# Attention and two feed-forward layers in float32 from float64 weights: the weight decode split over ScalarE and one VectorE step, decoded weights kept in PSUM

## The chip, the core and the metric

One core of a Trainium2 chip runs the whole program. Its engines work side by side and meet at semaphores: TensorE (PE, with its weight loads shown apart as PEld), VectorE (DVE), ScalarE (ACT), GpSimd (POOL) and SyncE (SP), which issues the transfers. Each engine runs its own list of instructions strictly in order. The metric is the device time of one execution in microseconds (us); lower is better.

## The reference, cut to what matters

```python
attn = softmax(causal(q @ k.T / 8)) @ v           # 2 batches x 12 heads x 448 x 64, float32
x    = attn as 896 tokens x 768
xn   = x / sqrt(mean(x*x) + 1e-6) * rms_g
x    = (silu(xn @ w_gate) * (xn @ w_val)) @ w_out          # 768 -> 1536 -> 768
h    = maximum(x @ w_in, 0)                                 # 768 -> 2048
out  = (h * h) @ w2_out                                     # 2048 -> 768
```

The five weight matrices arrive as float64: each number is a pair of 32-bit words, and the kernel has to make float32 of it on the chip. Activations are float32.

## The kernel before, in words

**Precision.** Every float32 operand of the large products is split into a rounded part (`high`, type float32r) and the rest (`low`), and three matmuls of 128x128 by 448 columns replace one. For an activation this is `parts` (L483 to L493: `high` through `rnd`, L198 to L204, `low` at L491); for a weight tile it is `form` (L591 to L607: `low` at L603), which writes a buffer of the pool `ring`.

**Decoding.** `weights` (L549 to L589) loads a tile of 128 x 768 float64 numbers as pairs of words into `raw` and makes float32 of it in `wt`, in four steps: `exponent` (L563 on ACT or L565 on POOL) reads the high word as a float32 and multiplies it by 2^-112; `sign` (L573 on DVE or L571 on POOL) writes the sign bit back into the high word's place; `upper` (L577, DVE) shifts the result left by three and puts the sign in; `lower` (L581, DVE) adds the top three bits of the low word.

**Products.** `product` (L609 to L621, the matmuls at L617) runs nine matmuls for a form of three 128-row blocks. Two column tiles of a weight matrix and the two batches make a 2x2 block product, done with seven products instead of eight: `differences` (L635 to L656, subtractions at L644) makes sums of activations, `minus` (L624 to L632, at L630) sums of weights, and `halves` (L658 to L699) runs one such pair of tiles: two `weights`, four `minus`, seven `form`, seven `product`, and the evictions in between (`snap` at L243 or L682, and `half_silu` at L711, `gated` at L734 or `squared` at L878). A pair has 63 matmuls. There are ten pairs for gate and value, then `layer` (L840 on) for the first output matrix, eight pairs for the second input matrix, and `layer` again for the last matrix.

**Order.** Nothing is issued in the order in which it is written. `Order` (L44 to L135) holds every step with its due time, the engines that may do it with an estimated duration each (functions A_, D_, P_, E_, L245 to L258), what it needs and which buffers it takes, and `run` plays it through: the step that could begin first is given to the engine with the lowest end plus a penalty (`COST`), and ties within `SLACK` go to the earliest due time. What comes out is one fixed list for each engine. Attention's twelve head pairs (`step`, L266 on) are due 6 us apart (`STRIDE`); the weights of the first tiles are decoded beside them. `norm` scales the finished rows (L540). PSUM is used by the attention pools until `banks_come`, after which eight banks `m` take the products.

## Time and profile before

| what | us |
|---|---|
| median of 3 runs (lowest, highest) | 655.7 (652.54, 658.22) |
| the profiled execution | 651.39 |
| its span, first to last instruction | 649.6 |
| PE busy | 582.8 (90% of the span) |
| DVE busy | 541.3 (83%) |
| POOL busy | 379.7 (58%) |
| ACT busy | 310.1 (48%) |
| mean granted TensorE clock | 0.963 of full |

Busy time is counted by engine over the whole span; what matters is which engine another waits for in each stage. On the page's chain of waits PE has 47% of the span and DVE 42%.

### The profile page before, as it was taken

The page shows a single profiled execution, that of the slowest core. Times are in us where ns is not written, and L with a number is a line of the kernel's source. Part 1 is how long each engine was busy: PE and PEld are TensorE (multiplying, and loading weights), DVE is VectorE, ACT ScalarE, POOL GpSimd, SP SyncE. Part 2 cuts the span into 40 slices and gives each one's busy share as a digit, 9 for nine tenths or more (in the row PEclk, how much of TensorE's full clock was granted, in tenths as well). Part 3 has the DMA queues.
Part 4 walks back from the last instruction along what each step waited for, and adds up shares of the span by engine and source line. Part 5 has one row for each costly group of instructions (what it writes and reads, how often), then busy time and mean ns, then how long its engine had stood idle before and what let it go on. Part 6 is the DMA issues. An engine that isn't in the chain of part 4 may idle for free.

```text
span 649.6 us, 8844 instructions
## 1 busy us (share of the span) xinstructions
PE 582.8 (90%) x3155; PEld 502.9 (77%) x3155; DVE 541.3 (83%) x668; ACT 310.1 (48%) x706; POOL 379.7 (58%) x373
## 2 busy tenths in 40 slices
PE   8998989509997899998899999889898899999997
PEld 5765657409986888787789998678787799999997
DVE  3678788892999999999997789999999999668521
ACT  4888676232454344544523336455555564435200
POOL 3569897571666765668644148767676788236100
PEclk9999999958999999999899999699899999999999
DMA  5365132100232333231345540023333222544111
GB/s 156 90 216 176 58 112 87 61 0 2 80 139 78 104 129 103 98 98 48 97 138 163 185 147 0 21 80 103 133 109 124 81 82 75 161 152 147 39 67 66
DMA packets 19500, 65.06 MB, mean 100 GB/s; under 512 B 2048, under 2 KB 8960, under 8 KB 19456
## 3 DMA queue, kind: packets, MB, share of 16 engines
q1 hardware_dynamic: 19456, 64.50, 30.7%
q8 instruction: 25, 0.41, 0.3%
q14 instruction: 19, 0.16, 0.1%
HBM read 61.74 MB, written 2.75 MB: 99 GB/s over the span
## 4 chain that ended last, share of the span: by engine, by line
PE 47%; DVE 42%; issue 7%; POOL 2%; DMA 1%; ACT 1%; SPq 0%; DVEq 0%; POOLq 0%; ACTq 0%
PE m L617 37%; DVE ring L603 8%; DVE wt L577 5%; DVE wt L581 5%; DVE sb L491 5%; PE s L297 2%; PE t L400 2%; DVE snap L644 2%; DVE fb L722 2%; DVE fa L540 2%; PE o L438 2%; DVE raw L573 2%; DVE st L630 2%; DVE mx L333 1%; PE s L800 1%
## 5 line engine op out<-in xcount | busy, mean ns | idle before, releaser
L617 PE MATMUL m<-sb,ring 128*128 128x448 f32 x1584 | 345.2, 374 | 46.0 <-DVE fa L745 23.3
L617 PEld LDWEIGHTS m<-sb,ring 128*128 128x128 f32 x1584 | 302.9, 193 | 79.7 <-ACT sb L202 23.7
L617 PE MATMUL m<-sa,ring 128*128 128x448 f32 x630 | 143.9, 375 | 6.8 <-DVE ring L603 3.0
L617 PEld LDWEIGHTS m<-sa,ring 128*128 128x128 f32 x630 | 120.9, 193 | 20.5 <-DVE ring L603 5.4
L202 ACT CAST ring<-wt 128x384 fp32r<-128x384 f32 (+1 forms) x107 | 51.6, 501 | 85.8 <-DVE wt L581 43.3
L577 DVE SCALAR_TENSOR_TENSOR wt<-wt,raw 128x768 uint32<-128x768 uint32 x70 | 82.7, 1181 | 5.8 <-POOL raw L571 3.7
L581 DVE SCALAR_TENSOR_TENSOR wt<-raw,wt 128x768 uint32<-128x768 uint32 x70 | 81.0, 1157 | 1.8
L603 DVE TENSOR_TENSOR ring<-wt,ring 128x384 fp32r<-128x384 f32 x77 | 57.7, 762 | 16.3 <-ACT ring L202 15.4
L563 ACT ACTIVATE wt<-raw 128x768 f32<-128x768 f32 (+1 forms) x55 | 48.7, 886 | 44.8 <-DMA raw<-in_w2o 14.9
L603 POOL TENSOR_TENSOR ring<-wt,ring 128x384 fp32r<-128x384 f32 (+1 forms) x45 | 54.3, 1210 | 20.2 <-ACT ring L202 18.9
L603 DVE TENSOR_TENSOR ring<-st,ring 128x384 fp32r<-128x384 f32 x47 | 42.6, 925 | 5.3 <-ACT ring L202 5.3
L630 POOL TENSOR_TENSOR st<-wt 128x384 f32<-128x384 f32 x17 | 19.6, 1157 | 40.3 <-DVE wt L581 39.7
L573 DVE TENSOR_SCALAR raw<-wt 128x768 uint32<-128x768 uint32 (+1 forms) x40 | 29.9, 747 | 15.2 <-ACT wt L563 13.5
L202 ACT CAST ring<-st 128x384 fp32r<-128x384 f32 x67 | 33.2, 511 | 19.2 <-PE m L617 15.2
L571 POOL TENSOR_SCALAR raw<-wt 128x768 f32<-128x768 f32 (+1 forms) x30 | 33.1, 1103 | 15.5 <-ACT wt L563 14.7
L603 POOL TENSOR_TENSOR ring<-st,ring 128x384 fp32r<-128x384 f32 x25 | 33.0, 1318 | 11.4 <-ACT ring L202 11.0
L333 DVE TENSOR_REDUCE mx<-s 128x2 f32<-128x256 f32 (+2 forms) x36 | 24.0, 685 | 17.4 <-PE s L301 10.7
L384 POOL TENSOR_SCALAR p<-p,r 128x128 f32<-128x128 f32 (+1 forms) x48 | 25.4, 547 | 18.8 <-DVE r L374 17.0
L243 ACT COPY snap<-m 128x448 f32<-128x448 f32 x39 | 20.1, 529 | 23.5 <-PE m L617 20.9
L384 POOL TENSOR_SCALAR p2t<-p2t,r 128x256 f32<-128x256 f32 (+1 forms) x36 | 25.9, 736 | 6.0 <-DVE r L374 5.6
L924 DVE TENSOR_TENSOR fb<-m,fb 128x448 f32<-128x448 f32 x12 | 7.5, 624 | 26.1 <-PE m L617 26.1
L297 PE MATMUL s<-qk 64*128 64x128 f32 (+2 forms) x144 | 27.5, 464 | 1.8 <-DMA qk<-in_qk 1.2
(132 smaller groups left out, 821.8 us busy)
## 6 DMA issues: line engine op xcount, KB each, us to landing
raw<-in_w2i SPq DMA_DIRECT2D x16, 768.0 KB, 4.2
raw<-in_wg SPq DMA_DIRECT2D x12, 768.0 KB, 4.6
raw<-in_wv SPq DMA_DIRECT2D x12, 768.0 KB, 4.6
raw<-in_wo SPq DMA_DIRECT2D x12, 768.0 KB, 4.3
raw<-in_w2o SPq DMA_DIRECT2D x12, 768.0 KB, 4.5
qk<-in_qk SPq DMA_DIRECT2D x11, 448.0 KB, 3.3
raw<-in_w2o SPq DMA_DIRECT2D x6, 512.0 KB, 3.8
out_t<-fb SPq DMA_DIRECT2D x12, 224.0 KB, 1.9
```

Source lines behind the costliest of these rows:

```text
L202: eng.copy(o, i)
L297: nc.tensor.matmul(s[:, h, o:o + n], z["qk"][BOTH[h], 0, qs], z["qk"][BOTH[h], 1, :n], start=True, stop=False)
L384: E(e).tensor_scalar(t, t, z["r"][:, k:k + 1], 1.0, ALU.mult, ALU.mult)
L491: E(e).tensor_sub(bs.tile[:, 1], bf.tile, bs.tile[:, 0].bitcast(F32))
L563: nc.scalar.activation(t, hi, AF.Copy, scale=2.0 ** -112)
L571: nc.gpsimd.tensor_scalar(s.bitcast(F32), t, 0.0, 1.0, ALU.mult, ALU.mult)
L573: nc.vector.tensor_scalar(s, t.bitcast(U32), 0x80000000, None, ALU.bitwise_and)
L577: nc.vector.scalar_tensor_tensor(u, u, 3, br.tile[:, :n * P, 1], ALU.logical_shift_left, ALU.bitwise_or)
L581: nc.vector.scalar_tensor_tensor(u, br.tile[:, :n * P, 0], 29, u, ALU.logical_shift_right, ALU.bitwise_or)
L603: E(e).tensor_sub(br.tile[:, 1, :n], num(), br.tile[:, 0, :n].bitcast(F32))
L617: nc.tensor.matmul(bank.tile[:, :S], bw.tile[:, a, i], x[:, c], start=first and i == 0 and k == 0, stop=last and i == n - 1 and k == 2, sk ...
L630: (E(e).tensor_add if plus else E(e).tensor_sub)(bs.tile, x, y)
```

## The change

The decode has three steps now, two of them on ACT. `exponent` is an ACT step with a two-slope function (Prelu): numbers below zero are multiplied by 2^32 times the scale, which leaves a bit pattern that, once shifted left by three, carries the sign. `lowest` (ACT) takes the top byte of the low word, turns it into the three bits that are wanted and writes them back to the low word's place. `number` (DVE) shifts and joins in one step. After attention, the decoded tile lies in a PSUM pool `w` (two buffers of two banks; the pool `m` goes from eight banks to four), and the second tile of a pair has its first half written to an SBUF buffer of pool `st`, so that no sum reads two PSUM operands. POOL reads no PSUM in this program, so steps that read `w` have lost POOL as an option. Steps that read two SBUF operands on DVE are marked `port`, and the planner lets none of them run beside a POOL step in its plan. The planner's durations, `COST`, `STRIDE` and the due times of evictions (`SOON`) differ; `differences` is due after the first tiles of batch 1 and writes rows of `fa`/`fb`; `half_silu` and `squared` work on the bank itself or take one DVE step for relu and square.

```diff
-STRIDE = 6.0
+STRIDE = 5.5
+SOON = 12.0
-COST = {"D": 1.0, "P": 0.6}
+COST = {"D": 0.3, "P": 0.6}
...
+                    if e == "P" or (e == "D" and t["port"]):
+                        b = max(b, free.get("port", 0.0))
...
+            if e == "P" or (e == "D" and t["port"]):
+                free["port"] = end
...
-    caps = dict(raw=2, wt=3, st=4, ring=8, snap=4, tt=2, uu=2, sa=6, sb=18, fa=14, fb=18, m=8)
+    caps = dict(raw=2, wt=2, st=5, ring=8, snap=4, tt=2, uu=2, sa=6, sb=18, fa=14, fb=18, m=4, w=2)
...
-        return 0.26 + 0.00085 * n + (ACC if acc else 0.0)
+        return 0.18 + 0.00085 * n + (0.08 + ACC if acc else 0.0)
...
-            if e == "A":
-                nc.scalar.activation(t, hi, AF.Copy, scale=2.0 ** -112)
-            else:
-                nc.gpsimd.tensor_scalar(t, hi, 2.0 ** -112, 1.0, ALU.mult, ALU.mult)
-        def sign(e):
...
-        def upper(e):
...
-        def lower(e):
...
+            nc.scalar.activation(bt.tile[:, :n * P], br.tile[:, :n * P, 1].bitcast(F32), AF.Prelu, scale=2.0 ** -112, alpha=2.0 ** 32)
+        def lowest(e):
+            b = br.tile.rearrange("p a b -> p (a b)").bitcast(U8).rearrange("p (a b) -> p a b", b=8)[:, :n * P, 3]
+            nc.scalar.activation(br.tile[:, :n * P, 0], b, AF.Copy, scale=1.0 / 32, bias=-31.0 / 64)
+        def number(a, b, dst=None):
+            def f(e):
+                u = bt.tile[:, a:b].bitcast(U32)
+                nc.vector.scalar_tensor_tensor(dst.tile.bitcast(U32) if dst else u, u, 3, br.tile[:, a:b, 0],
+                                               ALU.logical_shift_left, ALU.bitwise_or)
+            return f
...
-        t = chain(due, {"A": A_(w), "P": P_(w)}, exponent, [t], new=[bt], uses=[br], begin=begin)
-        t = add(due, {"P": P_(w), "D": 0.15 + w / 1700}, sign, [t], uses=[bt, br])
-        t = add(due, {"D": D_(w) + 0.02}, upper, [t], uses=[bt, br])
-        t = add(due, {"D": D_(w) + 0.08}, lower, [t], uses=[bt, br])
-        return bt, t
+        t1 = chain(due, {"A": A_(w)}, exponent, [t], new=[bt], uses=[br], begin=begin,
+                   **({"prev": [late["m"]]} if home == "w" else {}))
+        t2 = add(due, {"A": A_(w)}, lowest, [t], uses=[br])
+        if apart:
+            bs, h = buf("st"), w // 2
+            t = chain(due, {"D": D_(h)}, number(0, h, bs), [t1, t2], new=[bs], uses=[bt, br], port=home != "w")
+            return (bs, 0, t), (bt, h, add(due, {"D": D_(h)}, number(h, w), [t1, t2], uses=[bt, br], port=home != "w"))
+        return bt, add(due, {"D": D_(w)}, number(0, w), [t1, t2], uses=[bt, br], port=home != "w")
...
-        t = chain(due, {"A": A_(w), "P": P_(w)}, high, [t], new=[br], uses=[b])
-        return br, n, add(due, {"P": P_(w, True), "D": D_(w) + 0.05}, low, [t], uses=[b, br])
+        sb = b.pool != "w"
+        t = chain(due, {"A": A_(w), **({"P": P_(w)} if sb else {})}, high, [t], new=[br], uses=[b])
+        return br, n, add(due, {**({"P": P_(w, True)} if sb else {}), "D": D_(w)}, low, [t], uses=[b, br], port=sb)
...
-        k1 = snap(x, p1, due + 1.8)
-        done(0, 0, z, k1[0], [p2, k1[1]], due + 4)
+        k1 = snap(x, p1, due + 1.8 - SOON)
+        done(0, 0, z, k1[0], [p2, k1[1]], due + 4 - SOON, False)
...
+        def src():
+            return bf.tile if keep else bank.tile[:, :S]
         def whole(e):
-            nc.vector.tensor_add(bf.tile, bank.tile[:, :S], snap.tile)
+            nc.vector.tensor_add(src(), bank.tile[:, :S], snap.tile)
...
-        have(ctx.enter_context(tc.tile_pool(name="ps_m", bufs=8, space=PSUM)), "m")
+        have(ctx.enter_context(tc.tile_pool(name="ps_m", bufs=1, space=PSUM)), "m", "w")
...
-    f = differences(xf, 500.0)
+    f = differences(xf, 1012.0)
...
-        def relu(e):
-            nc.scalar.activation(bt.tile, bf.tile if snap else bank.tile[:, :S], AF.Relu)
-        def times(e):
-            E(e).tensor_mul(bf.tile, bt.tile, bf.tile if snap else bank.tile[:, :S])
+        def square(e):
+            nc.vector.scalar_tensor_tensor(bf.tile, bf.tile, 0.0, bf.tile, ALU.max, ALU.mult)
```

Over the whole program the lists hold 762 DVE instructions (670 before), 636 on ACT (624) and 195 on POOL (375); the matmuls are the same in number. The changed file's line numbers differ: L540, L491, L644, L603, L630, L716, L722, L739, L742 and L745 of before are L548, L499, L652, L608, L636, L733, L739, L755, L758 and L761 of the change, and the decode on DVE is L581 in it.

Two places of DVE's list, the engine that PE waits for in them. First, the end of attention: `fa` and `fb` are rows of activations, `sb` their split parts, `snap` a scratch row (before: also the differences), `s` the last attention banks. Before, the six scalings of `norm` (L540) and their first splits stand just ahead of these rows, which run to the step that frees the banks (L745):

```order
L644 TENSOR_TENSOR snap<-fa 128x448
L644 TENSOR_TENSOR snap<-fa,snap 128x448
L722 SCALAR_TENSOR_TENSOR fa<-tt,s 128x448
L491 TENSOR_TENSOR sb<-snap,sb 128x448 x2
L644 TENSOR_TENSOR snap<-fa 128x448
L491 TENSOR_TENSOR sb<-snap,sb 128x448
L644 TENSOR_TENSOR snap<-fa 128x448
L644 TENSOR_TENSOR snap<-fa,snap 128x448
L491 TENSOR_TENSOR sb<-snap,sb 128x448 x2
L644 TENSOR_TENSOR snap<-fa,snap 128x448
L491 TENSOR_TENSOR sb<-snap,sb 128x448
L745 SCALAR_TENSOR_TENSOR fa<-s,fa 128x448
```

The same place in the change, from the first scaling after the mean squares of batch 1 on; L761 is the step that frees the banks:

```order
L548 SCALAR_TENSOR_TENSOR fa<-fa,g_sb,snap 128x448 x3
L499 TENSOR_TENSOR sb<-fa,sb 128x448 x3
L548 SCALAR_TENSOR_TENSOR fa<-fa,g_sb,snap 128x448 x3
L499 TENSOR_TENSOR sb<-fa,sb 128x448 x3
L739 SCALAR_TENSOR_TENSOR fa<-tt,s 128x448
L761 SCALAR_TENSOR_TENSOR fa<-s,fa 128x448
L652 TENSOR_TENSOR fb<-fa,fb 128x448
L652 TENSOR_TENSOR fb<-fa 128x448
L608 TENSOR_TENSOR ring<-wt,ring 128x384 x2
```

The differences (L644, now L652) and their parts have moved from ahead of the step that frees the banks to behind it.

Second, DVE's list in the middle of the gate and value pairs. Before:

```order
L716 TENSOR_TENSOR fb<-m,snap 128x448
L722 SCALAR_TENSOR_TENSOR fb<-tt,m 128x448
L739 SCALAR_TENSOR_TENSOR uu<-m,snap 128x448
L722 SCALAR_TENSOR_TENSOR fb<-tt,fb 128x448
L630 TENSOR_TENSOR st<-wt,st 128x384
L742 TENSOR_TENSOR fb<-fb,uu 128x448
L716 TENSOR_TENSOR fb<-m,snap 128x448
L603 TENSOR_TENSOR ring<-wt,ring 128x384
L603 TENSOR_TENSOR ring<-st,ring 128x384 x3
L722 SCALAR_TENSOR_TENSOR fb<-tt,fb 128x448
L603 TENSOR_TENSOR ring<-wt,ring 128x384
L577 SCALAR_TENSOR_TENSOR wt<-wt,raw 128x768
```

The change, at such a place (the end of a value pair and the start of a gate pair):

```order
L581 SCALAR_TENSOR_TENSOR w<-w,raw 128x768
L755 SCALAR_TENSOR_TENSOR uu<-m,snap 128x448
L758 TENSOR_TENSOR fa<-fa,uu 128x448
L733 TENSOR_TENSOR m<-m,snap 128x448
L581 SCALAR_TENSOR_TENSOR st<-w,raw 128x384
L581 SCALAR_TENSOR_TENSOR w<-w,raw 128x384
L739 SCALAR_TENSOR_TENSOR fa<-tt,m 128x448
L608 TENSOR_TENSOR ring<-w,ring 128x384 x2
L636 TENSOR_TENSOR st<-st,w 128x384 x2
L636 TENSOR_TENSOR st<-w,st 128x384
L608 TENSOR_TENSOR ring<-st,ring 128x384 x2
L733 TENSOR_TENSOR fa<-m,snap 128x448
```

A tile takes one decode step here (or two of half its width), evictions (L733, L755) stand between the decode steps, and five of the seven sums and splits shown read `w`.

## Rows read from the trace of the kernel before

**Rows 1.** Windows by stage: us, busy (instructions) of PE, PEld, DVE, ACT, POOL; clock; DMA.

```profile
44.00:122.10 78.10, 70.60 (x590) 50.53 (x586) 65.40 (x111) 52.22 (x159) 60.80 (x79) 1.00 0.36 112
122.10:145.40 23.30, 0.00 (x0) 0.00 (x0) 23.08 (x22) 9.17 (x17) 18.94 (x15) 0.61 0.00 1
145.40:329.70 184.30, 169.23 (x782) 149.76 (x782) 169.29 (x194) 81.41 (x162) 112.66 (x95) 0.97 0.26 86
329.70:404.70 75.00, 75.00 (x369) 69.20 (x369) 61.63 (x68) 30.56 (x57) 33.93 (x30) 1.00 0.43 137
404.70:518.20 113.50, 99.06 (x435) 86.67 (x434) 112.42 (x123) 58.94 (x116) 81.08 (x62) 0.92 0.29 92
518.20:646.20 128.00, 127.95 (x630) 118.24 (x630) 83.42 (x96) 46.48 (x92) 49.98 (x42) 1.00 0.29 99
```

**Rows 2.** Waits of PE: waiting engine and line, releaser: us in total, times, longest.

```profile
PE m L617 <- DVE fa L882: 4.9, 3, 2.1
PE m L617 <- DVE fb L716: 4.2, 3, 3.1
```

**Rows 3.** Timeline of PE: start, us, instruction, count, idle before and its releaser.

```profile
119.14 2.96 PE L800 MATMUL s<-sa,ring 128*128 128x448 f32 x12
145.44 17.50 PE L617 MATMUL m<-sb,ring 128*128 128x448 f32 x72 [23.34 <-DVE fa L745]
...
209.66 7.12 PE L617 MATMUL m<-sb,ring 128*128 128x448 f32 x27 [3.11 <-DVE fb L716]
...
240.42 5.74 PE L617 MATMUL m<-sb,ring 128*128 128x448 f32 x27 [0.74 <-DVE fb L716]
...
416.46 7.35 PE L617 MATMUL m<-sb,ring 128*128 128x448 f32 x27 [1.92 <-ACT snap L243]
424.49 2.09 PE L617 MATMUL m<-sb,ring 128*128 128x448 f32 x9 [0.68 <-ACT snap L243]
```

**Rows 4.** Windows inside the gap after attention, columns as in rows 1.

```profile
124.00:126.00 2.00, 0.00 (x0) 0.00 (x0) 2.00 (x3) 0.56 (x1) 1.44 (x2) 1.00 0.00 0
126.00:128.00 2.00, 0.00 (x0) 0.00 (x0) 2.00 (x2) 0.58 (x2) 2.00 (x2) 0.84 0.00 0
```

**Rows 5.** Timeline of DVE in two gate and value pairs, columns as in rows 3.

```profile
231.10 1.36 DVE L603 TENSOR_TENSOR ring<-wt,ring 128x384 fp32r<-128x384 f32 x1
...
235.21 0.54 DVE L603 TENSOR_TENSOR ring<-wt,ring 128x384 fp32r<-128x384 f32 x1
235.68 0.95 DVE L577 SCALAR_TENSOR_TENSOR wt<-wt,raw 128x768 uint32<-128x768 uint32 x1
...
238.41 0.55 DVE L603 TENSOR_TENSOR ring<-st,ring 128x384 fp32r<-128x384 f32 x1
```

**Rows 6.** Groups by line and shape: count, busy us, mean ns of one, idle before.

```profile
L577 DVE SCALAR_TENSOR_TENSOR wt<-wt,raw 128x768 uint32<-128x768 uint32 x64 | 75.9, 1186 | 4.1 <-POOL raw L571 2.3
L581 DVE SCALAR_TENSOR_TENSOR wt<-raw,wt 128x768 uint32<-128x768 uint32 x64 | 74.2, 1160 | 1.6
L603 DVE TENSOR_TENSOR ring<-wt,ring 128x384 fp32r<-128x384 f32 x77 | 57.7, 762 | 16.3 <-ACT ring L202 15.4 <-POOL ring L200 0.7
L603 DVE TENSOR_TENSOR ring<-st,ring 128x384 fp32r<-128x384 f32 x47 | 42.6, 925 | 5.3 <-ACT ring L202 5.3
L573 DVE TENSOR_SCALAR raw<-wt 128x768 uint32<-128x768 uint32 x37 | 26.8, 725 | 15.2 <-ACT wt L563 13.5 <-POOL wt L565 1.6
L722 DVE SCALAR_TENSOR_TENSOR fb<-tt,fb 128x448 f32<-128x448 f32 x12 | 13.9, 1156 | 0.0
L716 DVE TENSOR_TENSOR fb<-m,snap 128x448 f32<-128x448 f32 x12 | 7.3, 612 | 0.0
L742 DVE TENSOR_TENSOR fb<-fb,uu 128x448 f32<-128x448 f32 x9 | 9.3, 1032 | 0.2
L563 ACT ACTIVATE wt<-raw 128x768 f32<-128x768 f32 x50 | 45.4, 907 | 41.3 <-DVE ring L603 12.6 <-DMA raw<-in_w2o 11.3 <-DMA raw<-in_wo 6.6
L202 ACT CAST ring<-wt 128x384 fp32r<-128x384 f32 x102 | 50.0, 511 | 85.8 <-DVE wt L581 43.3 <-PE m L617 42.4
```

More of the change, by code (lines that the diff above doesn't have):

```diff
@@ L62, in add, with chain @@
         return t
-    def chain(self, due, opts, f, after=(), new=(), **kw):
-        t = self.add(due, opts, f, after, new, prev=[self.last.get(b.pool) for b in new], **kw)
+    def chain(self, due, opts, f, after=(), new=(), prev=(), **kw):
+        t = self.add(due, opts, f, after, new, prev=[self.last.get(b.pool) for b in new] + list(prev), **kw)
         for b in new:
@@ L491, in low @@
             E(e).tensor_sub(bs.tile[:, 1], bf.tile, bs.tile[:, 0].bitcast(F32))
-        t = add(due, {"A": A_(S), "P": P_(S)}, high, [t], new=[bs], uses=[bf], prev=[late[bs.pool]])
-        return bs, add(due, {"P": P_(S, True), "D": 0.9}, low, [t], uses=[bf, bs])
+        t = add(due, {"A": A_(S), "P": P_(S)}, high, [t], new=[bs], uses=[bf], prev=[late[bs.pool], *prev])
+        return bs, add(due, {"P": P_(S, True), "D": D_(S)}, low, [t], uses=[bf, bs], port=True)
     def norm(b, due, gap):
@@ L544, in norm, with weights @@
             bx = pairs[b * NPAIR + i]["bx"]
-            xf[b][i] = (bx, add(due + gap * i, {"D": 0.75}, scaled(i), [s6], uses=[brb, bx]))
+            xf[b][i] = (bx, add(due + gap * i, {"D": D_(S)}, scaled(i), [s6], uses=[brb, bx], port=True))
             xs[b][i] = parts(xf[b][i], due + gap * i)
-    def weights(src, n, due, begin=0.0):
-        br, bt = buf("raw"), buf("wt")
+    def weights(src, n, due, begin=0.0, home="w", apart=False):
+        br, bt = buf("raw"), buf(home)
         def load(e):
@@ L630, in f @@
             (E(e).tensor_add if plus else E(e).tensor_sub)(bs.tile, x, y)
[L632 removed]
+        sb = "w" not in (a[0].pool, b[0].pool)
+        t = chain(due, {**({"P": P_(3 * P, True)} if sb else {}), "D": D_(3 * P)}, f, [a[2], b[2]], new=[bs],
+                  uses=[a[0], b[0]], port=sb)
         return bs, 0, t
@@ L776, in whole_tiles @@
                     else:
-                        t = product(banks[k], ws[2 * ft + k][i], xs[b][3 * i:3 * i + 3], due + ft, i == 0, i == 1)
+                        t = product(banks[k], ws[2 * ft + k][i], xs[b][3 * i:3 * i + 3], due + ft, i == 0, i == 1, [t])
                 if b:
@@ L849, in layer @@
                 for b in range(B):
-                    tt = product(banks[b], fm, x[b][k + o:k + o + m], due, first, c == len(chunks) - 1 and o + m == n)
-                    if c == len(chunks) - 1 and o + m == n:
-                        done(b, banks[b], tt, due)
+                    last = c == len(chunks) - 1 and o + m == n
+                    tt[b] = product(banks[b], fm, x[b][k + o:k + o + m], due, first, last, [tt[b]])
+                    if last:
+                        done(b, banks[b], tt[b], due - SOON)
                 first = False
@@ L859, in tile_attention_moe_moe2 @@
         for b in range(B):
-            hx[b][i] = parts(hf[b][i], due - 5 + i)
+            hx[b][i] = parts(hf[b][i], due - 5 + i, [x[1] for y in f.values() for x in y])
     yf = [[], []]
@@ L876, in tile_attention_moe_moe2, with squared, copied @@
     h2 = [[None] * NF2, [None] * NF2]
-    def squared(b, ft, bank, snap, after, due):
-        bf, bt = row(), buf("tt")
+    def squared(b, ft, bank, snap, after, due, keep=False):
+        bf = row()
         def whole(e):
             nc.vector.tensor_add(bf.tile, bank.tile[:, :S], snap.tile)
-        def relu(e):
-            nc.scalar.activation(bt.tile, bf.tile if snap else bank.tile[:, :S], AF.Relu)
-        def times(e):
-            E(e).tensor_mul(bf.tile, bt.tile, bf.tile if snap else bank.tile[:, :S])
-        r = None
+        def copied(e):
+            copy(e, bf.tile, bank.tile[:, :S])
+        def square(e):
+            nc.vector.scalar_tensor_tensor(bf.tile, bf.tile, 0.0, bf.tile, ALU.max, ALU.mult)
         if snap:
             r = add(due, {"D": D_(S)}, whole, after, new=[bf], uses=[bank, snap], prev=[late[bf.pool]])
-            after = [r]
-        t = add(due, {"A": A_(S)}, relu, after, new=[bt], uses=[bf if snap else bank])
-        t = add(due, {"P": P_(S, True), "D": 0.9} if snap else {"D": D_(S)}, times, [t], new=[] if snap else [bf],
-                uses=[bt] + ([bf] if snap else [bank]), prev=[] if snap else [late[bf.pool]])
+        else:
+            r = add(due, c2opt(S), copied, after, new=[bf], uses=[bank], prev=[late[bf.pool]])
+        t = add(due, {"D": D_(S)}, square, [r], uses=[bf])
         h2[b][ft] = (bf, t)
-        return r or t
+        return r
     for ft in range(0, NF2, 2):
```

110 lines of the change are left out of this document (53 added, 57 removed).

## The prediction

> **What bounds the kernel now.** I read the windows by stage first. Between 518.2 and 646.2 us, in the last layer, PE runs 630 matmuls in 128.0 us [rows 1], 0.2032 us each, and is busy for 127.95 of it. Between 329.7 and 404.7 it runs 369 in 75.0 us [rows 1], the same rate, with DVE busy for 61.6 us. Those stages are bound by PE, at its full granted clock, and nothing in them can be gained. Everything else is measured against 0.2032 us. From 145.4 to 329.7 (first tiles of batch 1 and the ten gate and value pairs) 782 matmuls would take 158.9 us and take 184.3 [rows 1]: 25.4 us lost. From 404.7 to 518.2 (end of the first output layer and the eight pairs of the second input matrix) 435 would take 88.4 and take 113.5 [rows 1]: 25.1 us lost. In the first of these stages DVE is busy for 169 of 184 us and in the second for 112.4 of 113.5 [rows 1], and the waits of PE there name DVE's evictions [rows 2]. Between them lies no other bound: these pairs run at DVE's pace. Third, from 122.1 to 145.4 PE has no instruction at all, while DVE is busy for 23.1 of 23.3 us [rows 1, 3]. Fourth, between 44 and 122 PE stands for 7.5 us of 78.1 [rows 1].
>
> The groups by shape tell why DVE is slow. An operation that takes one operand from a bank (L716) takes 612 ns for 448 columns, whatever POOL does; L742 and L722, with the same 448 columns and both operands in SBUF, take 1032 and 1156 ns [rows 6]. L603 shows the same inside one pair: 1.36 us at 231.1 and 0.54 at 235.2 [rows 5]. So reads of two SBUF operands are stretched at times, and 0.61 us (448 columns), 0.55 (384) and 0.95 (768) are the unstretched prices [rows 5, 6].
>
> **The change part by part.** The profiled execution took 651.4 us; the median of the runs is 655.7, 0.66% above it, and I carry that factor at the end.
>
> *DVE in a pair.* PE needs 63 x 0.2032 = 12.8 us for it. Before: two decodes of 1.186 + 1.160 and about 1.2 signs of 0.725 make 5.5; of seven `low` some 4.6 lie on DVE at about 0.81, 3.7; nearly two sums at 0.9, 1.6; evictions of a gate pair three at 0.61 and four gates at about 1.1, 6.2, of a value pair 4.6 [rows 6]. That is 17.0 and 15.4, 16.2 on average, and the timeline shows two pairs in 240.42 - 209.66 = 30.8 us, 15.4 each [rows 3]. The ledger is 5% too high, since instructions next to each other overlap. After: one decode of 768 columns and two of 384, 0.95 + 1.10 = 2.05; seven `low` and four sums at 0.55, 6.05; seven evictions and gates at 0.61, 4.3; 12.4 in all, 11.8 with the same 5%. I take 12.0.
>
> No row has a decode step that reads and writes a bank. Its ends are 0.95 [rows 5] and 1.19 us [rows 6]; I take 0.95, since L716's bank operand costs nothing extra.
>
> *ACT in a pair.* ACT is busy for 81.4 us in the gate and value stage [rows 1], about 8 us a pair. Two `lowest` and the share of exponents that POOL had come on top: 2.4 x 0.907 = 2.2 us if `lowest` costs what L563 does, the nearest row (same count, same spaced words) [rows 6]. Ends: 0.51 us each (L202) and twice 0.907. That is 10.2 us, 12.0 at worst, below PE's 12.8.
>
> *What a pair then costs.* With DVE at 12.0 of 12.8 PE sets the pace, but a list 94% full cannot hide each wait. The stage from 329.7 loses nothing with DVE 82% full; a pair of before needs 120% and loses 2.6 us. I take 0.5 us lost per pair, from ends of 0 and 2.6. Ten pairs leave 5 us and the start 1 of the first stage's 22.5 (25.4 less 2.9 of clock, below): **16.5 us gained**.
>
> *The gap after attention.* In 23.3 us DVE runs 22 instructions [rows 1], 1.05 us each because POOL runs subtractions beside them; only then L745 frees the banks. In the change six scalings, six splits, L739 and L761 stand there: 14, the first two or so ahead of the gap. At 0.61 and 1 us for ACT's share, less 1.8 us that lie ahead, the restart comes 7.9 us after 122.1 instead of 23.3; **15 us gained** (10 if all run at 1.05, 17 at best). The differences now lie behind 90 matmuls that need none of them (72 of batch 1 and the first two products of the first pair), 18 us of cover against some 20 DVE instructions, 12 us. If they slip, PE waits for the split of the first sum instead.
>
> *The clock.* The clock is still 1.00 in the window from 124 us, which begins 1.9 us after the last matmul, and falls to 0.84 in the next [rows 4]; at the restart 72 matmuls take 17.5 us for 14.6 [rows 3], 2.9 us lost at the lower level. A gap of some 5 to 8 us may still see it fall for a moment: **2 us gained**, 0 to 2.9.
>
> *The second transition.* From 404.7 to 424.49 PE runs 47 matmuls, 9.6 us of work, in 19.8 [rows 1, 3]; 27 of them take 7.35 us at a fallen clock [rows 3]. 10.2 us are lost to differences at contended prices. Uncontended they take half: 5 us left. The eight pairs behind it lose the other 14.9, 1.9 each; 0.5 each leaves 4. **16 us gained**; ends 8 (all of the transition stays, 1 us per pair) and 25.
>
> *Attention.* Some thirty copies of 512 columns go from ACT to DVE, about 0.7 us each, 20 us; seven two-step decodes of about 2.3 us and the stretched operations beside POOL go away, about as much. POOL, 60.8 us busy there [rows 1], keeps little besides the normalization. **4 us gained** of PE's 7.5; ends 7.5 and a loss of 3.
>
> *Edits taken at nothing.* Four product banks instead of eight: a pair takes three, the fourth starts the next pair, and the next is needed two products (3.7 us) later, when the first bank's eviction is long past; without that cover a 1.8 us product waits. Two `w` buffers instead of three `wt`: the next pair's exponents wait for this pair's last sum, with evictions and a `low` or two of 0.55 us to cover 0.91 of ACT. SP issues as many loads as before, and `raw` comes free sooner. The last layer stays bound by PE.
>
> Sum: 16.5 + 15 + 2 + 16 + 4 = 53.5. 651.4 - 53.5 = 597.9, times 1.0066: **602 us**.
>
> **The rivals.**
>
> *Cleaner (0.23).* A pair loses nothing (9 us), the start and the second transition 4 less: 597.9 - 13 = 585, **589 us** as a median. For it: evictions stand earlier in DVE's list, and it was late evictions that PE waited for [rows 2]. Against it: 94%.
>
> *DVE and ACT take turns at `w` (0.17).* ACT writes or reads the two `w` buffers five times per pair, two exponents and three roundings, 2 x 0.907 + 3 x 0.511 = 3.35 us [rows 6], among DVE's decodes, sums and splits of the same tile. If neither may use a buffer while the other does, DVE stands for part of that. Standing through 2.8 us makes DVE's pair 14.8: 2.0 us lost per pair instead of 0.5, 27 us more, **629 us**. For it: every decoded tile is rounded by ACT while sums on DVE read it. Against: no two engines work on one bank in the stages of before, so no row shows it, and ACT is free to run ahead. The Trainium skill ("PSUM — Partial Sum Buffer", section "PSUM bank collisions raise a hardware error") says that no two engines may touch the same PSUM bank and partitions at once, two reads included, and that software must keep them apart. By that rule the five visits exclude DVE, and the time is this rival's; without it, the forecast's. No trace here shows the rule yet.
>
> *Slower than before (0.04).* Evictions are due 12 us earlier, so DVE meets L733 or L755 between two decode steps, and its list stands until PE and `snap` are there; the decodes behind come late, PE runs short of forms, and both wait for each other. The gain is 53.5 us, so this decides when it costs over 3.4 us per pair: DVE standing 4.7 us in each, 0.67 per eviction. At 0.8 per eviction, 17.6 us a pair, 4.3 lost beyond the forecast in each of 18, **680 us**. Against it: PE's rate in the plan (1.83 us per product) is what the windows show, so plan and chip drift little.
>
> *It does not keep the reads apart (0.04).* The separation exists in the plan alone; nothing makes the chip wait. If the two or so POOL steps left per pair each stretch one DVE step by 0.5 us (1.156 against 0.61) and the next by as much, DVE needs 14 and a pair loses about 1 us: 9 us more, **611 us**.
>
> **How the numbers follow.** The forecast has 0.52, with its own range 590 to 613 from 0.2 to 0.9 us per pair and the ends of the transitions. The range of 8 in 10 reaches from 582, the cleaner case with attention's full gain, to 626, into the turns at `w`. A measurement of this kernel can tell about 1%, 6.6 us, from no change. Faster by more than that: forecast, cleaner, the unkept separation and nearly all of the turns, 0.93; within it 0.04, the turns with the lower ends of the other terms; slower 0.03.
>
> **What would show it.** Pairs: PE's rows a gate pair apart 26 to 27 us instead of 30.8 for two; DVE's splits at 0.55 in mean instead of 0.76 and 0.93; the decode near 0.95. The gap: 5 to 8 us. The second transition: half as long. The windows of the last layer as they are. Wrong, if ACT waits for DVE on `w` or DVE for ACT on it take more than a microsecond per pair; if `lowest` takes over 1.3 us; if PE waits for sums of activations behind those 90 matmuls.

## The result and the profile after

The change takes 584.6 us (median; 582.35 to 589.12) where the kernel before takes 655.9 beside it: a ratio of 0.893 (95% interval 0.885 to 0.900). Forecast were 602 us, in a range of 582 to 626; the time lies inside that range but below the forecast's own 590 to 613, and 4 us below the rival called cleaner (589). The profiled execution took 582.35 us, its span is 580.6 us, and on the chain of waits PE has 87% and DVE 7%, where they had 47% and 42%.

The windows by stage answer to [rows 1] and say where 69 us went. Columns: from and to in us, length, then busy us (instructions) of PE, PEld, DVE, ACT, POOL, granted clock, DMA share, GB/s. The stages are end of attention, gap, gate and value, first output layer, second input layer with its transition, last layer, and a steady piece of gate and value:

```profile
44.00:117.60 73.60, 68.47 (x584) 50.70 (x580) 62.90 (x124) 55.86 (x155) 41.47 (x61) 1.00 0.33 109
117.60:122.46 4.86, 0.00 (x2) 0.03 (x1) 4.83 (x10) 2.71 (x5) 0.00 (x0) 0.98 0.00 0
122.46:282.10 159.64, 157.95 (x770) 145.64 (x771) 141.35 (x256) 104.47 (x190) 24.73 (x31) 0.99 0.32 109
282.10:356.00 73.90, 73.90 (x366) 68.51 (x365) 37.18 (x60) 37.34 (x63) 5.30 (x6) 1.00 0.36 120
356.00:449.10 93.10, 91.58 (x452) 84.21 (x451) 87.96 (x151) 56.71 (x104) 21.93 (x25) 1.00 0.31 106
449.10:577.10 128.00, 128.00 (x632) 118.30 (x630) 60.48 (x98) 55.34 (x102) 14.94 (x15) 1.00 0.32 108
150.00:264.00 114.00, 113.25 (x558) 104.74 (x558) 104.03 (x190) 75.05 (x135) 16.77 (x24) 1.00 0.38 125
```

At 0.2032 us per matmul, 770 of them are 156.5 us: the gate and value stage loses 3.2 us where it lost 25.4. The second input stage loses 93.1 - 452 x 0.2032 = 1.3 us where it lost 25.1. The gap is 4.86 us instead of 23.3, and attention ends at 117.6 instead of 122.1. The sum is 22.2 + 23.8 + 18.5 + 4.5 = 69.0 us; the profiled executions differ by 69.0. The last layer is as it was.

The timeline of PE shows nearly all that it still waits for behind attention (start, us, instruction, count, idle before it and the releaser). It answers to [rows 3]:

```profile
122.46 16.30 PE L623 MATMUL m<-sb,ring 128*128 128x448 f32 x72 [4.86 <-DVE fa L761]
...
150.75 7.57 PE L623 MATMUL m<-sb,ring 128*128 128x448 f32 x36 [1.06 <-ACT snap L694]
...
264.74 2.09 PE L623 MATMUL m<-sb,ring 128*128 128x448 f32 x9 [0.63 <-ACT snap L694]
...
359.34 3.50 PE L623 MATMUL m<-sa,ring 128*128 128x448 f32 x16 [0.90 <-DVE ring L608]
...
368.93 9.39 PE L623 MATMUL m<-sb,ring 128*128 128x448 f32 x45 [0.61 <-DVE snap L251]
```

Between 158 and 264 PE never waits, through eight pairs; before, it waited seven times in that stretch ([rows 3] shows two of them). The second transition costs 0.90 + 0.61 us.

The groups by line and shape answer to [rows 6] (count, busy us, mean ns of one, idle before):

```profile
L581 DVE SCALAR_TENSOR_TENSOR w<-w,raw 128x768 uint32<-128x768 uint32 x41 | 39.3, 962 | 18.7 <-ACT w L571 10.5 <-ACT raw L576 8.2
L608 DVE TENSOR_TENSOR ring<-w,ring 128x384 fp32r<-128x384 f32 x105 | 56.0, 551 | 39.4 <-ACT ring L210 39.2
L608 DVE TENSOR_TENSOR ring<-st,ring 128x384 fp32r<-128x384 f32 x65 | 35.7, 573 | 9.0 <-POOL ring L208 5.6 <-ACT ring L210 3.1
L758 DVE TENSOR_TENSOR fa<-fa,uu 128x448 f32<-128x448 f32 x11 | 6.9, 625 | 0.4
L576 ACT ACTIVATE raw<-raw 128x768 uint32<-128x768 uint8 x64 | 58.3, 915 | 12.1 <-DMA raw<-in_wv 8.6 <-DMA raw<-in_w2i 1.2 <-DMA raw<-in_wo 1.2
```

The splits take 551 and 573 ns where they took 762 and 925, the product of gate and value 625 where it took 1032, and one decode step of 962 ns in PSUM replaces 1186 + 1160 and a sign.

DVE's timeline in the gap, the place of the first fence on the order:

```profile
113.34 2.78 DVE L548 SCALAR_TENSOR_TENSOR fa<-fa,g_sb,snap 128x448 f32<-128x448 f32 x3
116.05 1.69 DVE L499 TENSOR_TENSOR sb<-fa,sb 128x448 fp32r<-128x448 f32 x3
117.65 1.87 DVE L548 SCALAR_TENSOR_TENSOR fa<-fa,g_sb,snap 128x448 f32<-128x448 f32 x3
119.44 1.68 DVE L499 TENSOR_TENSOR sb<-fa,sb 128x448 fp32r<-128x448 f32 x3
121.05 0.61 DVE L739 SCALAR_TENSOR_TENSOR fa<-tt,s 128x448 f32<-128x448 f32 x1
121.69 0.62 DVE L761 SCALAR_TENSOR_TENSOR fa<-s,fa 128x448 f32<-128x448 f32 x1
```

Six of the fourteen steps lie ahead of 117.6, not two; the other eight make the 4.86 us.

### The profile page after: what moved, and what is told of

Read it like the earlier page. It is cut to its first block, busy times and chain, and to the rows that moved or that the text cites. A ratio compares the mean times of both kernels' runs of the same rounds, so it can differ in the third digit from the quotient of the medians.

```text
span 580.6 us, 8705 instructions
## 1 busy us (share of the span) xinstructions
PE 559.5 (96%) x3155; PEld 495.1 (85%) x3155; DVE 424.4 (73%) x760; ACT 340.9 (59%) x718; POOL 130.4 (22%) x193
## 4 chain that ended last, share of the span: by engine, by line
PE 87%; DVE 7%; POOL 2%; DMA 1%; ACT 1%; issue 1%; SPq 0%; POOLq 0%; DVEq 0%; ACTq 0%
PE m L623 73%; PE t L408 3%; PE o L446 3%; PE s L305 3%; POOL p L392 2%; DVE sb L499 2%; PE s L318 2%; PE s L817 1%; PE o L441 1%; DMA raw<-in_wg 1%; DVE mx L341 1%; DVE fa L548 1%; DMA qk<-in_qk 1%; DVE ring L608 1%; DVE fa L652 0%
## 5 line engine op out<-in xcount | busy, mean ns | idle before, releaser
L210 ACT CAST ring<-w 128x384 fp32r<-128x384 f32 (+1 forms) x111 | 49.6, 471 | 70.0 <-PE m L623 47.4
L608 DVE TENSOR_TENSOR ring<-w,ring 128x384 fp32r<-128x384 f32 (+1 forms) x111 | 57.6, 537 | 40.8 <-ACT ring L210 40.6
L576 ACT ACTIVATE raw<-raw 128x768 uint32<-128x768 uint8 x70 | 62.4, 894 | 12.1 <-DMA raw<-in_wv 8.6
L581 DVE SCALAR_TENSOR_TENSOR w<-w,raw 128x768 uint32<-128x768 uint32 x64 | 53.1, 831 | 20.9 <-ACT w L571 11.2
L208 POOL TENSOR_SCALAR ring<-st 128x384 fp32r<-128x384 f32 x23 | 12.1, 530 | 222.4 <-DVE st L636 124.4
L571 ACT ACTIVATE w<-raw 128x768 f32<-128x768 f32 x64 | 53.6, 850 | 12.7 <-DVE ring L608 9.3
L608 DVE TENSOR_TENSOR ring<-st,ring 128x384 fp32r<-128x384 f32 x65 | 35.7, 573 | 9.0 <-POOL ring L208 5.6
L210 ACT CAST ring<-st 128x384 fp32r<-128x384 f32 x49 | 24.7, 514 | 18.5 <-DVE st L636 14.7
L341 DVE TENSOR_REDUCE mx<-s 128x2 f32<-128x256 f32 (+2 forms) x36 | 24.0, 686 | 12.3 <-PE s L321 6.7
L392 POOL TENSOR_SCALAR p<-p,r 128x128 f32<-128x128 f32 (+1 forms) x48 | 24.0, 518 | 24.9 <-DVE r L382 18.4
L392 POOL TENSOR_SCALAR p2t<-p2t,r 128x256 f32<-128x256 f32 (+1 forms) x36 | 21.9, 625 | 11.0 <-DVE r L382 8.4
L366 ACT ACTIVATE p<-s,nb 128x128 f32<-128x128 f32 (+1 forms) x48 | 22.1, 473 | 1.3 <-ACT nb L346 0.4
L446 PE MATMUL o<-pt,vt 128*64 128x320 f32 (+2 forms) x192 | 20.2, 353 | 0.0
L408 PE MATMUL t<-ident,p 128*128 128x128 f32 x96 | 14.2, 283 | 5.8 <-POOL p L392 5.0
L251 ACT COPY fb<-m 128x448 f32<-128x448 f32 x21 | 11.1, 535 | 14.8 <-PE m L623 14.3
L499 DVE TENSOR_TENSOR sb<-fb,sb 128x448 fp32r<-128x448 f32 x29 | 19.6, 710 | 0.0
```

The costliest lines, as they stand in the source:

```text
L210: eng.copy(o, i)
L251: (nc.scalar.copy if e == "A" else nc.vector.tensor_copy)(o, i)
L392: E(e).tensor_scalar(t, t, z["r"][:, k:k + 1], 1.0, ALU.mult, ALU.mult)
L408: nc.tensor.transpose(t[:, i * P:(i + 1) * P], src[:, o * P:(o + 1) * P], ident)
L446: nc.tensor.matmul(z["o"][BOTH[h], S - n:S], z["v"][:, j, h * D:(h + 1) * D], z["pt"][:, h, KO[j]:KO[j] + n], start=j == 0, stop=j == 3)
L499: E(e).tensor_sub(bs.tile[:, 1], bf.tile, bs.tile[:, 0].bitcast(F32))
```

## The experiments

The theory at the start: each part (short decode, weights in PSUM, early evictions, reads kept apart, late sums of activations) takes DVE work or DVE delay off PE's path, and a pair loses nothing once DVE's list is shorter than PE's 12.8 us. The chief rival: one part does it all. Five kernels undo parts (e4 two of them at once), two add work to DVE, one puts the decode alone into the kernel before; the last ones try for more. The expectations take work per pair as DVE's busy time in the window from 150 to 264 us, over that window's matmuls, times 63; in the change it is 104.03 / 558 x 63 = 11.75 us. In some of the runs that window begins in the first pair, with its waits and its lower clock, and the figure comes out too high. So the windows below hold six whole pairs each, 378 matmuls from the start of a pair's first one, and work per pair is a sixth of DVE's busy time. First the change, then e1:

```profile
165.45:242.06 76.61, 76.61 (x380) 71.01 (x378) 70.27 (x130) 50.57 (x91) 8.71 (x13) 1.00 0.36 124
175.77:253.89 78.12, 78.12 (x380) 70.95 (x379) 70.17 (x129) 53.51 (x98) 1.89 (x2) 1.00 0.40 132
```

A pair of the change takes 12.77 us and 11.7 of DVE, 92% of it.

**e1: decoded weights in SBUF.** `home = "wt"` everywhere, `caps` with wt=3, st=4; the steps on them may go to POOL again and count as `port`.

> The changed kernel with decoded weights kept in SBUF (pool wt, three buffers) instead of PSUM; POOL is allowed again as an option and the planner's separation applies to these steps. Theory (DVE's work per pair, 11.75 us against PE's 12.8, sets whether PE waits): the decode step costs 0.95 us from SBUF too, and the plan keeps POOL away, so DVE stays under 12.8 and the time stays within 580 to 592 us. Rival (the bank operand is what keeps DVE's steps unstretched): splits of weights go back to 0.76 us and above, a pair takes 14 us or more, 605 us or more.

599.2 us, 0.913 of before (0.905 to 0.920): between the two. In the steady pairs PE is not held up, and DVE's 11.7 us are the same as in the change. The rival's reason fell: splits of `wt` take 551 ns from 150 to 264 us. PE's waits stand at the start, a gap of 6.1 us and 2.88 us for DVE behind it. That attention ends 3.4 us later belongs to the execution, as e9, the same kernel as the change, ends it 3.2 us later. One rounding on POOL, at 152.46 us, takes 5.51 us while DVE's steps run back to back beside it; the two others of its group in that window take 0.51 us each.

Of the 14.5 us to the change a part is no wait at all but a slower pitch of the matmuls (last section); the placement's own price stays uncertain. Against e9's profile, whose attention ends as late and whose pairs run at the same pitch, e1's is 12.9 us longer: some 8 of them stand at the gap, the first pair and the second transition, the rest in the pitch of the output layers.

**e2: reads not kept apart.**

```
-                    if e == "P" or (e == "D" and t["port"]):
+                    if False:
```

> The changed kernel with the planner no longer keeping POOL's steps and DVE's two-SBUF-operand steps apart; its list then holds 256 POOL instructions instead of 193 and 722 on DVE instead of 762. Theory: some 60 more POOL steps each stretch one or two DVE steps by 0.5 to 0.9 us, 30 to 55 us of DVE time, against 23 us that DVE hands over; DVE comes to 12 to 13.4 us per pair and the time to 585 to 600 us. Rival (the separation is worth nothing): 585 us with DVE less busy. Rival (the separation is most of the gain): over 615 us.

593.2 us, 0.905 (0.900 to 0.910): the time is as expected, the place is not. DVE needs 11.2 us per pair (100.17 / 561 x 63), less than the 12 to 13.4 expected and less than in the change, and PE waits once in that window, for 0.38 us. The gap is 8.89 us, with the same steps in it as in the fence above (timeline of DVE):

```profile
117.79 3.61 DVE L548 SCALAR_TENSOR_TENSOR fa<-fa,g_sb,snap 128x448 f32<-128x448 f32 x3
121.32 3.91 DVE L499 TENSOR_TENSOR sb<-fa,sb 128x448 fp32r<-128x448 f32 x3
```

Three scalings take 3.61 us instead of 1.87, three splits 3.91 instead of 1.68: POOL runs beside them. So the plan's separation does its work on the chip, at the transitions. It is worth these 4 us, and in the second input stage 3.8 us of waits stand where the change has 1.5, the first of them (1.84 us for ACT's `snap`) with 27 matmuls in 7.38 us behind it.

**e3: evictions late.** `SOON = 0.0`.

> The changed kernel with evictions due when they were before (SOON = 0). Theory: DVE's work is the same, so PE waits little, 583 to 592 us. Rival (it was the earlier evictions that took PE's waits away, not DVE's smaller work): PE waits for evictions again by 1 to 3 us per pair, 600 to 640 us.

603.4 us, 0.919 (0.914 to 0.924): the theory fell here, and the rival held, at 0.9 us per pair where it had 1 to 3. Window of six pairs and timeline of PE:

```profile
168.25:250.35 82.10, 78.07 (x379) 70.52 (x378) 69.64 (x129) 50.95 (x92) 8.82 (x11) 1.00 0.36 120
```

```profile
187.24 2.09 PE L623 MATMUL m<-sb,ring 128*128 128x448 f32 x9 [0.63 <-ACT snap L694]
...
194.64 5.63 PE L623 MATMUL m<-sb,ring 128*128 128x448 f32 x27
200.89 2.09 PE L623 MATMUL m<-sb,ring 128*128 128x448 f32 x9 [0.62 <-ACT snap L251]
202.82 1.98 PE L623 MATMUL m<-sa,ring 128*128 128x448 f32 x9
```

PE waits once per pair and a pair takes 13.66 us (187.24 to 200.89), though DVE needs only 69.64 / 6 = 11.6 us for it, as in the change. The wait names ACT's copy of a bank (`snap`), but ACT is not late: it has been idle for 0.81 us when PE's product ends, and begins at once (ACT, then DVE):

```profile
200.31 0.53 ACT L251 COPY snap<-m 128x448 f32<-128x448 f32 x1 [0.81 <-PE m L623]
200.94 0.61 DVE L761 SCALAR_TENSOR_TENSOR fa<-m,fa 128x448 f32<-128x448 f32 x1
```

What is different is PE's own list. `halves` runs seven products, p1 to p7. Four of them (p1, p6, p7, p4) add up in one bank, which is copied between each two of them. In the change p6, p5 and p7 follow each other, and p5 covers the copy. Here p7 stands directly behind p6 (200.89), and p2 (202.82) and p5 come after it. p2 needs a free bank of the four, and the last eviction of the pair before gives it one. In the change that eviction, L761, begins 0.2 us after its product p4 (PE: p4 and p3, then p2, then p6, p5 and p7; the second row is DVE's):

```profile
189.16 3.81 PE L623 MATMUL m<-sb,ring 128*128 128x448 f32 x18
191.19 0.62 DVE L761 SCALAR_TENSOR_TENSOR fa<-m,fa 128x448 f32<-128x448 f32 x1
192.81 1.99 PE L623 MATMUL m<-sa,ring 128*128 128x448 f32 x9
194.63 5.63 PE L623 MATMUL m<-sb,ring 128*128 128x448 f32 x27
```

In e3 p4 is the first of the 27 matmuls' three products, and its eviction begins 4.5 us after it, at 200.94. In the plan p2 has no bank yet when p7 could begin, so p7 goes first. Little work on DVE is not enough: an eviction that stands behind other steps in its engine's list keeps a bank back, and with it the products that would have covered a copy.

**e4: the old decode, in SBUF, in the new plan.** The four steps of before, with `port` where they read SBUF; otherwise as e1.

> The changed kernel with the four-step decode of before, in SBUF; planner, order and all else as changed. Theory: DVE has two steps of 0.95 us (or more) per tile and part of the signs instead of one, 1.9 to 3 us more per pair, 13.6 to 14.8 us against PE's 12.8; 18 pairs lose 0.8 to 2 us each, 600 to 625 us. Rival (the decode was not what held PE; order and separation were): below 592 us.

616.9 us, 0.941 (0.936 to 0.946), 17.7 us more than e1:

```profile
174.18:256.45 82.27, 78.39 (x380) 70.52 (x378) 79.22 (x136) 44.08 (x84) 12.74 (x12) 1.00 0.35 114
```

DVE needs 79.22 / 6 = 13.2 us per pair and PE gets a pair done in 13.7 (197.92 to 211.63). The time is as the theory has it, but the wait that PE shows in these pairs is like that of e3, 0.62 to 0.68 us for ACT's copy, and a pair is as long as there, where DVE has 11.6 us. Here p4 stands directly behind p7: in the plan the form of the next pair's first product, which stands between them in the change, is not ready, as DVE has the longer decode to do. So the decode is what costs, but by way of PE's order, and how much of the 17.7 us DVE's pace by itself would cost, this run does not tell.

**e5: sums of activations early.** `differences(xf, 500.0)` instead of 1012.0.

> The sums of activations are due at 500 again, before the step that frees the attention banks. Theory (the gap after attention is the number of DVE steps that stand ahead of the freeing step): some 33 DVE and POOL steps come back ahead of it, the gap goes from 4.9 to 15 to 20 us and the restart runs part of its matmuls at the lower clock, 1 to 2 us more; 598 to 604 us. Rival (the gap was long because of stretched reads, not because of the order of steps): the planner keeps the reads apart, the gap stays below 9 us, 584 to 589 us.

595.8 us, 0.910 (0.906 to 0.914), 2 us under the expected range. The mechanism is as the theory has it:

```profile
135.40 17.38 PE L623 MATMUL m<-sb,ring 128*128 128x448 f32 x72 [17.13 <-DVE fa L761]
```

The gap is 17.1 us with reads kept apart, and 1.1 us more go to the clock. The first pair then finds its sums ready: PE's 1.06 us of wait for it vanish. The range's lower end was also set too high, since 10 us of gap and 1 of clock, the lower ends of its own terms, give 596. So of the gap's 18.5 us, 12.3 come from the order of the steps; the other 6.2 belong to the rest of the change, and e2 gives 4 of them to the separation.

**e6 and e7: more work for DVE.** Two and four of a pair's seven `low` steps are done twice (the same value written again).

```
         t = add(due, {..., "D": D_(w)}, low, [t], uses=[b, br], port=sb)
+        if twice:
+            t = add(due, {"D": D_(w)}, low, [t], uses=[b, br], port=sb)
```

> Two of a pair's seven low steps are done twice on DVE, 0.55 us each more, so DVE needs 12.85 us per pair for PE's 12.8. Theory (PE sets the pace and DVE's 11.75 us fit under it whole; PE is late as soon as DVE needs more than 12.8): between +1 us (0.05 per pair) and +10 us (0.5 per pair in 18 pairs, waits that a full list no longer hides): 585 to 595 us. Rival (DVE's work is not what limits a pair; the order of evictions is): 583 to 587 us here and with four.

> Four of a pair's seven low steps are done twice on DVE: 13.95 us per pair for PE's 12.8. Theory: at least 1.15 us per pair in 18 pairs, 21 us, and 0.5 more for each if waits come on top: 605 to 615 us, with DVE busy over 95% in the middle pairs. Rival (DVE's work does not limit a pair): 583 to 590 us.

592.8 us (0.906; 0.901 to 0.910) and 609.2 us (0.929; 0.924 to 0.934): both in the theory's ranges. The windows of six pairs, of e6 and then of e7:

```profile
170.11:248.23 78.12, 78.12 (x379) 70.96 (x378) 71.77 (x137) 51.23 (x94) 7.51 (x11) 1.00 0.37 122
```

```profile
176.95:257.97 81.02, 78.88 (x379) 70.58 (x378) 78.41 (x150) 49.49 (x91) 5.42 (x8) 1.00 0.35 118
```

With two, DVE has 12.0 us per pair, not the 12.85 that were aimed at, and PE waits for nothing from 156 to 260 us; the added 8 us lie at the start, where PE waits 2.9 us for sums, forms and an eviction, at the second transition, and in the pitch. So e6 came into its range by other ways than the theory's, and as its pairs run at the slower pitch (13.02 us), its DVE is 92% busy, no more than the change's. With four, DVE has 13.1 us per pair, and PE waits for it every second pair (timeline of PE in e7):

```profile
200.49 1.68 PE L626 MATMUL m<-sa,ring 128*128 128x448 f32 x7 [0.64 <-DVE ring L608]
202.01 5.63 PE L626 MATMUL m<-sb,ring 128*128 128x448 f32 x27
...
215.18 5.74 PE L626 MATMUL m<-sb,ring 128*128 128x448 f32 x27
...
227.56 1.69 PE L626 MATMUL m<-sa,ring 128*128 128x448 f32 x7 [0.64 <-DVE ring L608]
```

Two pairs take 27.07 us (200.49 to 227.56), 13.53 each, and DVE is busy for 97% of the window. So at 12.0 us of DVE a pair costs PE nothing, and at 13.1 DVE holds PE up. What a list between 92% and 97% full costs was not measured.

**e8: the decode alone, in the kernel before.** Three steps instead of four, in SBUF, with the old planner, order and costs.

> The kernel before with the three-step decode alone, decoded weights in SBUF, the old order of evictions and differences, the old planner. Theory (before, DVE's work set the pace of the pairs): DVE per pair falls from 15.4 to some 12 us, the two stages bound by DVE gain 35 to 45 us, the gap after attention stays at 20 to 23 us: 610 to 622 us. Rival (late evictions keep PE waiting whatever DVE has to do, as when the evictions' due times alone are put back): pairs near 13.7 us, 630 to 645 us.

616.6 us, 0.940 (0.934 to 0.945), as the theory has it:

```profile
189.83:268.42 78.59, 77.53 (x379) 70.83 (x378) 72.50 (x94) 51.34 (x91) 44.02 (x40) 1.00 0.39 127
```

PE waits once in this window (0.93 us), the pairs of the second input matrix take 12.85 us, and the gap stays at 22.2 us. By itself the decode is worth 38.7 of the 71 us. The rival, late evictions, does no harm here. That is not for want of work on DVE: it has 12.1 us per pair, more than e3's 11.6, though POOL takes 7.3. There are eight banks `m` here and four in e3, and in PE's list another product stands between every two that share a bank in these pairs, but for the one wait. So the early evictions seem to be needed because of the four banks; eight banks with late evictions in the new plan were not run.

**e9: the change again.** Run beside e10 and e11.

> The changed kernel again, as the measure for the two kernels beside it: 582 to 589 us. A second question: where no engine makes PE wait, do its matmuls follow each other at 0.203 us throughout, as in the changed kernel's profile, or at 0.207, as in long stretches of the profiles of e1, e2 and e6? If the pitch goes with the kernel, 0.203 again; if it goes with the execution, 0.207 in some stretch that begins after a wait.

583.5 us, 0.891 (0.887 to 0.895). The pitch goes with the execution (last section), and so do some 3 us of attention: it ends at 120.8 here, at a granted clock of 0.96 to 0.97 in its first 100 us (1.00 in the change's profile), with the gap at 4.86 us again.

**e10: banks freed before the norm's steps.** The freeing steps of the first tiles are due ahead of everything, the gate's as soon as its own bank is done; `banks_come` waits for them and the norm alone; batch 1's first tiles run over `i` outermost.

```
-                half_silu(b, ft, banks[0], None, [t], due + ft)
+            half_silu(b, ft, banks[0], None, [ts[0]], -10.0 + ft)
-    ... used_ps + [x[1] for b in xs for x in b])
+    ... used_ps + [xf[1][0][1]])
```

> The two steps that free the attention banks are due before the scalings and splits of batch 1 (the first of them as soon as the gate's bank is done), the banks wait for nothing else, and the first tiles of batch 1 run over the upper three rows in all four banks first. Theory (the gap after attention is the DVE work that stands ahead of the freeing step, and the clock falls only in a gap that long): the freeing step ends near 118.5 us, the gap is about 1 us instead of 4.9, the restart runs at the full clock (72 matmuls in 14.8 us instead of 16.3): 4 to 6 us off, 579 to 581 us. Rival (what is freed earlier is lost behind it, as PE then comes to the first pair before its forms and sums are there): gap 1 us, but the first pair waits 3 to 5 us more, 583 to 586 us.

587.9 us, 0.897 (0.893 to 0.900): the gap is 0.81 us as expected, the time is not. PE pays ahead of it (timeline of PE):

```profile
117.64 0.89 PE L819 MATMUL s<-sa,ring 128*128 128x448 f32 x3 [0.63 <-ACT tt L736]
119.31 2.69 PE L819 MATMUL s<-sa,ring 128*128 128x448 f32 x12 [0.78 <-DVE fa L739]
122.81 15.11 PE L623 MATMUL m<-sb,ring 128*128 128x448 f32 x72 [0.81 <-DVE fa L761]
```

Both banks of a tile are one buffer, so PE's next bank waits while ACT and DVE read the first, and the matmuls behind attention end at 122.0. Behind it the first pair waits 1.47 + 0.69 us, as the rival has it, and at the second transition PE waits 2.34 us for ACT's copy, where the change waits 1.5 in all. The time is above the rival's range too: the first pair begins at 150.6, as in the change's profile (150.8), and not all of the 4 us to e9 is accounted for.

**e11: and ACT shares attention's normalization.** L392 may run on ACT as well.

> As the kernel with the early banks, and ACT may do the normalization of attention's rows as well as POOL (the planner gives it 16 steps of 84). Theory (PE's 5 us of waits for POOL in attention are POOL's queue): half of them go, attention ends 2 us earlier, 577 to 580 us. Rival (ACT's copies and exponentials come later by as much): 580 to 584 us.

584.2 us, 0.891 (0.887 to 0.894), no better than the change. PE's waits for POOL fall from 5 us to 1.1, but it now waits for DVE's maxima and ACT's exponentials instead, 2.5 us between the banks of the first tiles as in e10, and 2.55 us at the first pair.

**e12: and the gate's bank is read when both are done.** `[t]` instead of `[ts[0]]`.

> As the kernel with the early banks and ACT's share of the normalization, but the first freeing steps wait until both attention banks of a tile are done, as in the changed kernel, so that PE is not held up between a tile's two banks (2.5 us of waits for ACT and DVE inside the first tiles, in the profile of e11). Theory: these waits go, the gap becomes 2 to 2.5 us (one tanh and two DVE steps) at the full clock, attention ends 1 us earlier: 580 to 582.5 us. Rival (the first pair's start is set by ACT's and DVE's lists there, wherever PE is before it): PE's wait at the first pair grows by what is gained ahead of it, and the time stays at 583 to 585 us.

581.5 us, 0.886 (0.882 to 0.889): the lowest time, but its interval overlaps that of the change (e9), 2 us or 0.3% apart. Attention ends at 116.2, the gap is 2.66 us, the first pair waits 0.86 us, so the rival fell. The theory's clock fell too:

```profile
118.83 16.39 PE L626 MATMUL m<-sb,ring 128*128 128x448 f32 x72 [2.66 <-DVE fa L764]
```

```profile
116.00:118.00 2.00, 0.17 (x1) 0.00 (x0) 2.00 (x4) 1.02 (x3) 0.00 (x0) 1.00 0.00 0
118.00:120.00 2.00, 1.17 (x4) 1.10 (x5) 1.97 (x5) 0.56 (x2) 0.00 (x0) 0.79 0.04 8
120.00:122.00 2.00, 2.00 (x7) 1.78 (x6) 0.41 (x1) 0.00 (x0) 0.00 (x0) 0.50 0.00 0
```

## Why the prediction was right, and where it was off

**The bound: right.** Gate and value pairs and those of the second input matrix ran at DVE's pace. e8 takes decode work off DVE alone, and both stages come loose, at 13.1 and 12.85 us per pair where they took 15.1 and 14.9. e7 puts DVE at 13.1 us per pair, and PE waits for its splits again.

**DVE in a pair: right.** 11.8 by the ledger and 12.0 taken; 11.7 measured. `number` costs 962 ns with a bank as operand and as result, 0.95 was taken; `lowest` 915 ns, 0.907 was taken. ACT needs 50.57 / 6 = 8.4 us per pair where 10.2 were forecast: the 8 us of before counted the first tiles' share, and without it they are 81.41 / 782 x 63 = 6.6. It changes nothing, as ACT was under PE's pace either way.

**What a pair then costs: the mis-sized step.** "A list 94% full cannot hide each wait", 0.5 us per pair. Measured: nothing, in eight pairs on end, with a list 92% full; e6's is no fuller, so a list of 94% was never tried. That is 9 of the 15.5 us by which the sum (53.5) fell short of 69.0. The reason given for the 0.5 was the fill of the list; e3 shows a wait that comes of the place of steps in it. There DVE has the same 11.6 us of work and PE waits 0.63 us per pair; with evictions 12 us earlier nothing waits. This was written down for the cleaner rival ("evictions stand earlier"), at 0.23.

**The gap: right in kind, 3.5 us too small.** e5 shows that the sums of activations make 12.3 us of it. 7.9 us were forecast to remain (14 x 0.61 + 1 - 1.8, its own terms, give 7.7), 4.86 did, because six steps lie ahead of PE's end, not two. The clock's 2 us were 1.2: it still falls around the restart (72 matmuls in 16.30 us).

**The second transition: mis-sized, and half misread.** The prediction put the 10.2 us of before to differences at contended prices. PE's waits among them are 1.80 + 0.71 + 1.92 + 0.68 = 5.1 us; the rest is matmuls at a lower clock, 0.50 from 408 to 414 us:

```profile
404.70:424.49 19.79, 14.68 (x49) 12.06 (x48) 19.72 (x19) 7.78 (x16) 15.37 (x11) 0.74 0.12 41
```

5 us were left in the forecast by halving, 1.3 are left in the whole stage: the waits fell to 0.90 + 0.61, and the clock stays at 1.00 in that stage. e2, with 3.8 us of waits there and 27 matmuls in 7.38 us, says that the separation matters here.

**Attention: the number came out, 4.5 us for 4, but not by the reason given.** PE's waits for POOL there are 5.2 us before and 5.3 after, and all its waits up to the end of attention 10.3 and 9.3. The rest is PE's busy time for the same matmuls, 111.5 and 108.1 us. In e9 the same kernel ends attention only 1.3 us earlier than before. That the term fits is luck.

**The edits taken at nothing: right with the change's evictions.** Four banks `m` cost nothing in the change. In e3, where evictions come late, a product has to wait for one of them in the plan, and PE waits for a copy in each pair.

**Turns at `w`: refuted as a price.** The rival asked for 2.8 us per pair of DVE standing. The waits of DVE from 150 to 264 us (waiting engine and line, releaser: us, times, longest):

```profile
DVE w L581 <- ACT w L571: 0.9, 1, 0.9
```

That is 0.9 us in nine pairs. ACT waits 7.3 us for DVE's decoded tile there, 0.8 per pair, but that is data that it needs, and under the microsecond that was to show this rival. The rule that the prediction cited (the Trainium skill, "PSUM — Partial Sum Buffer", section "PSUM bank collisions raise a hardware error") asks that the engines be kept apart; these waits are how the program does it, and in a list ordered like this one they cost PE nothing. What an access without them would do, no run here shows.

**Slower by early evictions: refuted.** DVE's waits for PE at evictions (L755, L733, L761) come to 4.0 us in nine pairs, 0.45 per pair, where 4.7 were the point of decision. **Unkept separation: refuted** by the splits' 551 and 573 ns, with few exceptions (three products of gate and value on rows `fb` average 945 ns from 150 to 264 us).

What is left open: the parts undone one by one cost 17.7 (decode, e4 against e1), 14.5 (placement), 8.6 (separation), 18.8 (evictions) and 11.1 us (sums of activations), 71 together. That they add up to the whole is no proof that they are independent: the decode alone is worth 38.7 in the kernel before (e8), and medians differ by a few us through the pitch. The price of the placement in SBUF is the least certain of them. `COST`, `STRIDE`, the planner's durations and the shorter relu-and-square were not undone by themselves.

## What to carry to other kernels

Cost an engine's list in two ways: its work per period, which has to be under the pace of the engine it feeds (92% was still free here, 97% was not), and the place in it of each step that frees a buffer, which can cost the engine behind it a wait per period at the same work. Steps that free a resource go ahead of steps that only prepare. And before a gap is attacked, look at what the next stage will want: e10 and e11 closed it from 4.9 to 0.8 us and gained nothing, since the waits came back on either side.
